# Unscaled keys in a delta-rule recurrence, one written order for all engines, and other places for loads and transposes

## The chip, the core and the metric

The kernel runs on one core of a Trainium2 chip. The core has five engines with a queue of instructions each, worked off in order: TensorE (PE) for matrix products and transposes, VectorE (DVE), ScalarE (ACT) and GpSimd (POOL) for elementwise work, and SyncE (SP), which here does nothing but start transfers (DMAs). An engine that waits holds everything that stands behind in its queue. Matrix products are written to PSUM, eight banks of 2 KB per partition; everything else lies in SBUF. The metric is the device time of one execution in microseconds (us).

## The reference

Two blocks follow each other. The first is a delta-rule attention (4 batches, 8 heads, 768 steps, 48 dimensions per head), the second a feed-forward block with SiLU on 3072 tokens (384 to 2048 to 384). The two weight matrices come as 64-bit floats, all else as 32-bit floats.

```
k_n = k / (np.linalg.norm(k, axis=-1, keepdims=True) + 1e-06)
for t in range(S):
    kt, vt, bt = (k_n[:, :, t], v[:, :, t], beta[:, :, t, None])
    y[:, :, t] = np.einsum('bhd,bhde->bhe', q[:, :, t], state)
    v_old = np.einsum('bhde,bhd->bhe', state, kt)
    state = state + bt[:, :, :, None] * np.einsum('bhd,bhe->bhde', kt, vt - v_old)
...
x = np.ascontiguousarray(attn_out.transpose(0, 2, 1, 3)).reshape(B * S, H * D)
h = x @ w_in
g = h * (1.0 / (1.0 + np.exp(-h)))
return (g @ w_out).astype(np.float32)
```

## The kernel before

**Tiling.** The 768 steps are cut into 6 chunks of 128. A unit is one batch of one chunk (24 units, numbered chunk by chunk): 128 steps on the partitions, 8 heads of 48 dimensions beside each other, padded to 64. For each chunk c the kernel runs these stages over the four units:

- `norms(c)`: ACT squares the keys, DVE sums them and computes the inverse norm by Newton steps (13 small operations on 128x32).
- `scale(i)`: POOL multiplies the keys of unit i by the inverse norm (`kb`) and the result by -beta (`bkb`). POOL has no access to PSUM.
- `turn(i)`: PE transposes `kb` and `qb` (4 transposes each, tile `pt`), DVE and ACT copy them to `kq`.
- `score(i)`: PE multiplies keys by keys and queries (`pa`, 8 matmuls), ACT copies and DVE masks the results, with the scale -beta, to `ap`.
- `block_out(i)`, `block_in(i)`: the 32x32 blocks on the diagonal of the scores go to DRAM and come back regrouped (`g`, 128 blocks on the partitions).
- `invert(c)`: a recurrence on DVE inverts all 128 triangular blocks at once: POOL selects the part above the diagonal of `g` into `x`, and 30 steps of two operations (`rank`, `x`) follow; then the results go through DRAM (`up`, `low`) to the tiles `xe` and `xi`.
- `solve(c)`: PE merges the 32x32 inverses to 64x64 (`py`, `px`), solves for the new values (`pz`, first half, across, second half), updates the state (`pu`) and forms the attention output (`pyc`). ACT and DVE move results between PSUM and SBUF in each step (`y`, `xi`, `z`, `vf`, `xT`).
- `feed_forward(c)`: `hidden` (`phid`, 6 matmuls per step, SiLU to `gT` on ACT) and `project` (`po`, 16 matmuls per batch), both over the finished chunk. `go(pieces, n)` puts n small pieces of it between steps of the next chunk's stages.

**Weights.** Each of the two matrices is fetched raw in eight pieces of 0.79 MB into rooms that are free for the moment (`fetch_w_in`, `fetch_w_out`). `narrow` turns the 64-bit words of a piece to 32-bit floats: ACT takes Abs and Identity of the two halves, DVE does three operations, and POOL adds. A queue of pieces and `fill(n)` spread these operations over the first chunk. The raw pieces of `w_out` 2, 3, 6 and 7 share buffers (tag `ap`) with the scores.

**Order.** A scheduler would order the queues by itself. Two helpers bind it: `in_line` chains all DMAs on SP in program order, and `pin` chains an engine's operations in program order, but only once the engine stands in `pins`: for DVE, PE and POOL after the first weight pieces, for ACT never. `busy` is a matmul without use (`pw`), run so that PE is not idle.

**Start.** SP loads beta, 4 key units and 3 query units, then four pieces of `w_in` between the block transfers of chunk 0. Pieces 4 to 7 follow the first loads of v and are in flight during `invert(0)`. The keys of chunk 1 are loaded behind `invert(0)`, their norms and transposes come during and after `solve(0)`.

The lines below carry the numbers that the profile uses.

Of the kernel before, what the change touches and what calls it, by code (L numbers as in the profile page):

```python
# [21 lines left out]
def kernel(  # L22
# [9 lines left out]
):  # L32

# [9 lines left out]
    nc = tc.nc  # L43
# [42 lines left out]
    def pin(op):  # L86


        engine = op.ins.engine
        if engine in pins:  # L90
            behind(op, pins[engine])
            pins[engine] = op
        return op
# [13 lines left out]
    NQ, NK, NBK = 3, 2, 5  # L107
# [3 lines left out]
    kfs, vfs, invs = {}, {}, {}  # L111
# [8 lines left out]
    def load_k(i):  # L120
        if i < N:
            kfs[i] = load.tile([P, H, D], FP32, name="kf", bufs=5)
            in_line(nc.sync.dma_start(out=kfs[i][:], in_=chunk_of(k, i)))
# [11 lines left out]
    pin(nc.vector.memset(seen[:], 0.0))  # L135
    states = [const.tile([P, NP, 2 * W], FP32, name=f"state{b}") for b in range(B)]
    pin(nc.vector.memset(states[B - 1][:], 0.0))
    for t in qbufs:
        pin(nc.vector.memset(t[:, :, :, D:W], 0.0))
    beta_fm = work.tile([BH, S], FP32, name="beta_fm", tag="ap", bufs=4)  # L140
    in_line(nc.sync.dma_start(out=beta_fm[:], in_=beta.rearrange("b h s -> (b h) s")))
    for load_one, i in (
        *((load_k, i) for i in range(B)), *((load_q, i) for i in range(NQ)),
    ):
        load_one(i)
# [104 lines left out]
    for t in kbufs + bkbufs:  # L250
        nc.gpsimd.memset(t[:, :, :, D:W], 0.0)
# [14 lines left out]
    zbufs = [const.tile([P, NP, 2, W], FP32, name=f"z{i}") for i in range(3)]  # L266
# [17 lines left out]
    nc.scalar.activation(out=seen[:], in_=seen[:], func=ACTF.Silu)  # L284

    beta_tok = const.tile([P, NCH, BH], FP32, name="beta_tok")
    turned = None
    for c in range(NCH):
        if c < NCH - 2:
            turned = busy(turned)  # L290
        pb = bank(psM, "m", "pb")
        last = turned
        turned = nc.tensor.transpose(
            pb[:, 0:BH], beta_fm[:, c * C : (c + 1) * C], ident[0:BH, 0:BH]
        )
        if last is not None:
            behind(turned, last)
        pin(nc.scalar.activation(
            out=beta_tok[:, c, :], in_=pb[:, 0:BH], func=ACTF.Copy, scale=-1.0
        ))  # L300


    def norms(c):

        def one(name, dtype=FP32):
            return small.tile([P, BH], dtype, name=name, bufs=1)[:]

        ss = one("ss")
        for b in range(B):
            sq = work.tile([P, H, D], FP32, name="sq", bufs=1)  # L310
            pin(nc.scalar.activation(out=sq[:], in_=kfs[c * B + b][:], func=ACTF.Square))
            pin(nc.vector.tensor_reduce(
                out=ss[:, b * H : (b + 1) * H], in_=sq[:], axis=AX.X, op=ALU.add
            ))
        seed, t, r = one("seed", U32), one("nt"), one("nr")
        inv = small.tile([P, B, H], FP32, name="inv")
        pin(nc.vector.tensor_scalar(
            out=seed, in0=ss.bitcast(U32), scalar1=-0.5, scalar2=1597463007.0,
            op0=ALU.mult, op1=ALU.add,
        ))  # L320
        root = seed.bitcast(FP32)
        for _ in range(3):
            pin(nc.vector.scalar_tensor_tensor(
                out=t, in0=ss, scalar=-0.5, in1=root, op0=ALU.mult, op1=ALU.mult
            ))
            pin(nc.vector.tensor_tensor(out=t, in0=t, in1=root, op=ALU.mult))
            pin(nc.vector.scalar_tensor_tensor(
                out=r, in0=t, scalar=1.5, in1=root, op0=ALU.add, op1=ALU.mult
            ))
            root = r  # L330
        pin(nc.vector.tensor_tensor(out=t, in0=r, in1=ss, op=ALU.mult))
        pin(nc.vector.tensor_scalar(
            out=t, in0=t, scalar1=1e-6, scalar2=-1.0, op0=ALU.add, op1=ALU.mult
        ))
        pin(nc.vector.reciprocal(out=inv[:].rearrange("p b h -> p (b h)"), in_=t))
        for b in range(B):
            invs[c * B + b] = inv[:, b, :]
# [5 lines left out]
    def scale(i):  # L343

        b, c = units[i]
        kb, bkb = kbufs[i % NK], bkbufs[i % NBK]
        bt = beta_tok[:, c, b * H : (b + 1) * H]
        pin(nc.gpsimd.tensor_tensor(  # L348
            out=packed(kb), in0=kfs.pop(i)[:],
            in1=invs.pop(i).unsqueeze(2).to_broadcast([P, H, D]), op=ALU.mult,  # L350
        ))
        scaleds[i] = pin(nc.gpsimd.tensor_tensor(
            out=packed(bkb), in0=packed(kb), in1=bt.unsqueeze(2).to_broadcast([P, H, D]),
            op=ALU.mult,
        ))

    def turn(i, rooms):

        kb, bkb, qb = kbufs[i % NK], bkbufs[i % NBK], qbufs[i % NQ]
        if i not in scaleds:  # L360
            scale(i)
        scaled = scaleds.pop(i)
        kq = work.tile([P, NP, 2, C], FP32, name="kq", bufs=4)
        for j, (src, room) in enumerate(zip((kb, qb), rooms)):
            pt = bank(*room, "pt")
            for p in range(NP):
                pin(nc.tensor.transpose(  # L367
                    pt[:, p * C : (p + 1) * C], src[:, p].rearrange("p e w -> p (e w)"), ident[:]
                ))
            ptv = pt[:].rearrange("p (a t) -> p a t", a=NP)  # L370
            if j == 0:
                pin(nc.vector.tensor_copy(out=kq[:, :, j, :], in_=ptv))  # L372
            else:
                pin(nc.scalar.copy(kq[:, :, j, :], ptv))  # L374
        return dict(kq=kq, bkb=bkb, scaled=scaled)

    def score(i, u, rooms):

        b, c = units[i]
        kq, bt = u["kq"], beta_tok[:, c, b * H : (b + 1) * H]  # L380
        ap = work.tile([P, H, 2, C], FP32, name="ap", tag="ap", bufs=4)
        u["ap"] = ap
        for g, room in enumerate(rooms):
# [29 lines left out]
            u["ends"] = (copied, masked, u["scaled"])  # L413
            yield

    def block_out(i, u):
# [3 lines left out]
        if b == 0:  # L420
            blocks[c] = (
                tc.dram_tile([B, H, NB, T, T], FP32, name=f"blocks{c}"),
                work.tile([P, T, T], FP32, name="g", tag="g", bufs=1),
                work.tile([P, T, T], FP32, name="x", tag="x", bufs=1),
            )
        there = blocks[c][0]
# [12 lines left out]
    def invert(c):  # L439
# [4 lines left out]
        pin(nc.gpsimd.affine_select(  # L444
            out=x[:], in_=g[:], pattern=[[-1, T], [1, T]], compare_op=ALU.is_gt, fill=0.0,
            base=0, channel_multiplier=0,
        ))
        diagonal = x[:].rearrange("p s t -> p (s t)")[:, 0 : T * T : T + 1]
        yield pin(nc.vector.memset(diagonal, 1.0))
# [35 lines left out]
    def solve(c, us):  # L485
# [8 lines left out]
        def z_of(x):  # L494
            return zbufs[(c * B + x) % len(zbufs)]
# [157 lines left out]
        for k in range(B + 3):  # L653
# [3 lines left out]
            if k >= 3:  # L657
                old(k - 3)
                made = [update(k - 3), new(k - 3)]
                for part in made:  # L660
                    next(part, None)
# [12 lines left out]
            for part in made:  # L674
                next(part, None)
# [56 lines left out]
    def prepare(c, us):  # L732

        for b in range(B):
            i = c * B + b
            us.append(turn(i, (A, CC)))
            yield
# [5 lines left out]
            load_k(i + B)  # L743
            yield

    norms(0)
    fetch_w_in(0)
    us = [turn(0, (M, M))]
    load_q(B - 1)
    fetch_w_in(1)  # L750
    for b in range(B):
        if b + 1 < B:
            us.append(turn(b + 1, (M, M)))
        go(score(b, us[b], (CC, A)), 3)
        block_out(b, us[b])
        if b < 2:
            fetch_w_in(2 + b)
# [3 lines left out]
    ends = us[B - 1]["ends"]  # L761
# [28 lines left out]
    begun = fill(5)  # L790
    for op in begun:
        for end in ends:
            if end.ins.engine == op.ins.engine:
                behind(op, end)
    quiet = us[B - 1]["last"]
    for _ in range(16):
        quiet = busy(quiet, NoSync)
    for engine, op in (("vector", begun[-1]),):
        pins[op.ins.engine] = op
    pins[quiet.ins.engine] = quiet  # L800
    pins[adds[-1].ins.engine] = adds[-1]

    for i in range(B):
        load_v(i)
    for i in range(4, NWI):
        fetch_w_in(i)
    fetch_w_out(0)
    for n, done in enumerate(invert(0)):
        if n == 18:
            for i in range(20):  # L810
                busy(done if i == 0 else None, Sync)
# [13 lines left out]
    fill(7)  # L825
    for n in range(B, 2 * B):
        load_k(n)
    more(1, ("in", 1))
    pieces = feed_forward(0)
    for n, _ in enumerate(solve(0, us)):  # L830
        fill(2)
        if n == 5:
            norms(1)
            scale(B)
        if n == 3:
            for i in range(B, B + NQ):
                load_q(i)
            more(2)
            more(3)
        if n == 7:  # L840
            scale(B + 1)
        if n == 8:
            more(4, ("out", 1))
        for _ in range((2, 2, 1, 1, 1, 1, 1)[n] if n < 7 else 0):
# [8 lines left out]
    next_us = []  # L853
# [3 lines left out]
    for n in range(4):  # L857
        go(prep)
        go(pieces, 2)
        fill(3)  # L860
        if n % 2 == 0:
            scale(B + 2 + n // 2)
    for n in range(2):
        until(("out", 6 + n))
        for _ in range(2):
            go(prep)
            go(pieces)
    inv = invert(1)
    for _ in range(20):
# [5 lines left out]
    for n, _ in enumerate(solve(1, us)):  # L875
        go(pieces, 2 if n in (1, 2) else 1)
    norms(2)
# [5 lines left out]
    for c in range(1, NCH):  # L883
        if c + 1 < NCH:
# [13 lines left out]
            if c + 2 < NCH:  # L898
                norms(c + 2)
# [35 lines left out]
```

## Time and profile before

| | us |
|---|---|
| five runs | 801.94, 803.23, 798.36, 801.18, 801.08 |
| median | 801.18 |
| the profiled execution, its own time | 801.94 |
| its span, first to last instruction | 800.2 |
| PE busy | 764.1 (95%) |
| DVE / ACT / POOL busy | 338.6 / 224.1 / 85.4 |
| mean granted clock of PE | 0.98 |
| chain that ended last: PE, issue, DMA, DVE | 86%, 4%, 4%, 2% |
| PE phid / po on that chain | 31% / 30% |

How to read it: the busy time of an engine is the time in which one of its instructions runs; a matrix product overlaps the load of the next weights (PEld), and products are pipelined. One product of 32-bit floats can be two instructions in the trace. The granted clock is the share of full speed at which PE was let run; stretches of it below 1 are slow whatever stands in PE's queue. The chain of waits is followed back from the last instruction to whatever released each step, and printed in order of time. In a timeline, the bracket behind a row gives the idle time of the engine before it and what ended it. Times are counted from the span's start.

### The profile page before, as it was taken

The page shows a single profiled execution, that of the slowest core. Times are in us where ns is not written, and L with a number is a line of the kernel's source. Part 1 is how long each engine was busy: PE and PEld are TensorE (multiplying, and loading weights), DVE is VectorE, ACT ScalarE, POOL GpSimd, SP SyncE. Part 2 cuts the span into 40 slices and gives each one's busy share as a digit, 9 for nine tenths or more (in the row PEclk, how much of TensorE's full clock was granted, in tenths as well). Part 3 has the DMA queues.
Part 4 walks back from the last instruction along what each step waited for, and adds up shares of the span by engine and source line. Part 5 has one row for each costly group of instructions (what it writes and reads, how often), then busy time and mean ns, then how long its engine had stood idle before and what let it go on. Part 6 is the DMA issues. An engine that isn't in the chain of part 4 may idle for free.

```text
span 800.2 us, 15363 instructions
## 1 busy us (share of the span) xinstructions
PE 764.1 (95%) x6344; PEld 573.9 (72%) x6344; DVE 338.6 (42%) x871; ACT 224.1 (28%) x482; POOL 85.4 (11%) x96
## 2 busy tenths in 40 slices
PE   7919798999999999999999999999999999999998
PEld 4505586678768678868778868778868778768684
DVE  3678788392245642325642325642325642100000
ACT  3604437212235113224113225113214113211020
POOL 6003355100020000020000020000020000000000
PEclk9959899999999999999999999999999999999999
DMA  8795536503025140025140025140022040000000
GB/s 156 136 203 149 132 117 160 102 11 95 6 66 104 39 102 2 12 60 104 39 102 3 11 61 103 34 102 8 10 61 52 13 111 4 10 21 1 20 1 20
DMA packets 155061, 50.84 MB, mean 64 GB/s; under 512 B 142544, under 2 KB 147536, under 8 KB 154992
## 3 DMA queue, kind: packets, MB, share of 16 engines
q1 hardware_dynamic: 154992, 49.87, 28.3%
q8 instruction: 50, 0.82, 0.4%
q14 instruction: 19, 0.16, 0.1%
HBM read 34.70 MB, written 14.16 MB: 61 GB/s over the span
## 4 chain that ended last, share of the span: by engine, by line
PE 86%; issue 4%; DMA 4%; DVE 2%; ACT 1%; SPq 1%; POOL 1%; ACTq 0%; DVEq 0%; POOLq 0%
PE phid L687 31%; PE po L707 30%; PE pa L388 5%; PE pz L551 3%; PE pyc L610 3%; PE pt L367 3%; PE pyc L582 2%; PE ph L535 2%; PE pu L593 2%; PE py L518 1%; PE px L518 1%; DMA w_out<-in_moe_w_in_dram 1%; PE pz L559 1%; DMA raw_out<-in_moe_w_out_dram 1%; DVE rank L454 1%
## 5 line engine op out<-in xcount | busy, mean ns | idle before, releaser
L687 PE MATMUL phid<-xT,w_in 128*128 128x256 f32 x1152 | 266.5, 383 | 0.0
L707 PE MATMUL po<-w_out,gT 128*128 128x384 f32 x768 | 254.6, 489 | 0.0
L687 PEld LDWEIGHTS phid<-xT,w_in 128*128 128x128 f32 x1152 | 213.1, 190 | 35.4 <-issue 6.5
L707 PEld LDWEIGHTS po<-w_out,gT 128*128 128x128 f32 x768 | 144.1, 190 | 96.4 <-issue 1.2
L697 ACT ACTIVATE gT<-phid 128x512 f32<-128x512 f32 x96 | 57.3, 597 | 162.0 <-PE phid L687 162.0
L404 DVE SCALAR_TENSOR_TENSOR ap<-pa,beta_tok,above 128x128 f32<-128x128 f32 x192 | 58.2, 377 | 51.4 <-ACT ap L398 51.4
L275 PE MATMUL pw<-state,ident 128*128 128x384 f32 x98 | 41.6, 572 | 22.2 <-DVE x L458 17.2
L454 DVE TENSOR_TENSOR rank<-g,x 128x30 f32<-128x30 f32 (+9 forms) x180 | 59.7, 332 | 6.1
L458 DVE TENSOR_TENSOR x<-x,rank 128x30 f32<-128x30 f32 (+9 forms) x180 | 59.6, 331 | 6.3 <-DVE rank L454 0.2
L348 POOL TENSOR_TENSOR kb<-kf,inv 128x384 f32<-128x384 f32 x24 | 20.2, 842 | 364.1 <-PE po L707 240.3
L713 ACT ACTIVATE o<-po 128x384 f32<-128x384 f32 x24 | 11.8, 490 | 158.1 <-PE po L707 158.0
L388 PE MATMUL pa<-kq 48*128 48x256 f32 x384 | 49.6, 394 | 4.3 <-ACT kq L374 3.5
L398 ACT ACTIVATE ap<-pa,beta_tok 128x128 f32<-128x128 f32 x144 | 41.5, 367 | 31.4 <-PE pa L388 31.4
L388 PEld LDWEIGHTS pa<-kq 48*128 48x128 f32 x384 | 36.4, 189 | 16.0 <-issue 7.5
L275 PEld LDWEIGHTS pw<-state,ident 128*128 128x128 f32 x98 | 19.9, 216 | 34.8 <-issue 20.8
L551 PEld LDWEIGHTS pz<-vf,xi 64*64 64x64 f32 x768 | 37.0, 137 | 10.6 <-issue 7.8
L542 DVE TENSOR_TENSOR vf<-vf,pz 64x384 f32<-64x384 f32 x24 | 13.4, 558 | 73.4 <-PE pz L551 31.5
L551 PE MATMUL pz<-vf,xi 64*64 64x48 f32 x768 | 41.5, 222 | 1.4 <-DVE vf L542 1.3
L542 DVE TENSOR_TENSOR vf<-vf,ph 128x384 f32<-128x384 f32 x20 | 11.1, 554 | 51.6 <-PE ph L535 51.3
L372 DVE COPY kq<-pt 128x512 f32<-128x512 f32 x24 | 16.4, 683 | 35.9 <-PE pt L367 35.8
L569 ACT COPY z<-pz 64x384 f32<-64x384 f32 x48 | 22.7, 472 | 31.6 <-PE pz L551 17.5
L559 PE MATMUL pz<-z,ap 64*64 64x48 f32 x384 | 27.8, 223 | 0.0
(98 smaller groups left out, 588.1 us busy)
## 6 DMA issues: line engine op xcount, KB each, us to landing
kf<-in_k_dram SPq DMA_DIRECT2D x24, 192.0 KB, 3.1
qb<-in_q_dram SPq DMA_DIRECT2D x24, 192.0 KB, 3.5
vf<-in_v_dram SPq DMA_DIRECT2D x24, 192.0 KB, 3.5
out_dram<-o SPq DMA_DIRECT2D x24, 192.0 KB, 1.9
blocks<-ap SPq DMA_DIRECT2D x96, 32.0 KB, 1.7
g<-blocks SPq DMA_DIRECT2D x24, 128.0 KB, 2.7
up<-x SPq DMA_DIRECT2D x6, 512.0 KB, 2.6
low<-g SPq DMA_DIRECT2D x6, 512.0 KB, 2.8
```

The costliest lines, as they stand in the source:

```text
L275: done = pin(nc.tensor.matmul(pw[:, 0:DM], lhsT=ident[:], rhs=states[B - 1][:].rearrange("p a w -> p (a w)")[:, 0:DM], start=True, stop=Tr ...
L388: u["last"] = pin(nc.tensor.matmul(pa[e][:, pp * 2 * C : (pp + 1) * 2 * C], lhsT=kq[rows, 2 * g + pp, 0, :], rhs=kq[rows, 2 * g + pp, :, : ...
L398: copied = pin(nc.scalar.activation(out=ap[:, h, 0, :], in_=pa[e][:, at : at + C], func=ACTF.Copy, scale=bt[:, h : h + 1],))
L404: masked = pin(nc.vector.scalar_tensor_tensor(out=ap[:, h, j:2, :], in0=pa[e][:, at + j * C : at + 2 * C].rearrange("p (j t) -> p j t", j= ...
L454: pin(nc.vector.tensor_tensor(out=tv, in0=g[:, 0:m, m : m + 1].to_broadcast([P, m, n]), in1=x[:, m : m + 1, m + 1 : T].to_broadcast([P, m, ...
L458: yield pin(nc.vector.tensor_tensor(out=x[:, 0:m, m + 1 : T], in0=x[:, 0:m, m + 1 : T], in1=tv, op=ALU.add))
L542: pin(nc.vector.tensor_tensor(out=vs[x][rows], in0=vs[x][rows], in1=what[rows], op=ALU.add))
L551: yield pin(nc.tensor.matmul(pzs[x][rows, h, :], lhsT=xis[x // HB][rows, x % HB * H + h, :], rhs=vs[x][rows, h, :], start=True, stop=True,))
L559: yield pin(nc.tensor.matmul(pzs[x][hi, h, :], lhsT=us[x]["ap"][lo, h, 0, W:C], rhs=z_of(x)[lo, h // 2, h % 2, 0:D], start=True, stop=True,))
L687: pin(nc.tensor.matmul(ph[:, j * GT : (j + 1) * GT], lhsT=w_in[:, a, (2 * f + j) * P : (2 * f + j + 1) * P], rhs=xTs[c, hf][:, a, :], star ...
L697: pin(nc.scalar.activation(out=gTs[f // FG][:, f % FG, :], in_=ph[:], func=ACTF.Silu, scale=0.5))
L707: pin(nc.tensor.matmul(po[:, 0:DM], lhsT=gTs[f // 2 // FG][:, f // 2 % FG, at : at + C], rhs=w_outs[f // HFF][:, f % HFF, :], start=(f == ...
```

## The change

The keys stay unscaled. With n the norm (plus 1e-6) and g = -beta/n², the scores of raw keys are scaled by g; the state and the solved values are those of the scaled problem times n, so v is multiplied by n (`size`, POOL), the keys by g for the update (`scale`, POOL), and q enters with the sign turned. Transposes then need only the loaded keys, which are loaded straight into padded buffers (`kbufs`, five; `qbufs`, four; `zbufs`, four, which also hold the squares).

All engines are pinned from the first instruction, ACT included. Chunk 0 starts with three `busy` matmuls and the transposes of two units; beta of chunk 0 alone is transposed there. In `invert`, POOL fills `x` with zeros and ones ahead of time, and three copies on DVE and two on ACT bring in the part of `g` that the first steps need, in the place of POOL's selection and a write of the diagonal.

SP has a new order: all of chunk 0's keys and queries, `w_in` pieces 0 and 1, the blocks of chunk 0 without a break, then the keys of chunk 1, pieces 2 and 3, the queries of chunk 1, v, the transfers of `invert(0)`, and only then pieces 4 to 7. The betas of chunks 1 to 5 and the transposes of chunk 1 stand on PE in `invert(0)`, ahead of the 20 `busy` matmuls; for chunks 0 and 1 ACT alone copies them to `kq`. `squares(1)` and `norms(1)` follow `invert(0)` directly instead of running in `solve(0)`. In `solve`, the products `pu` and `pyc` of a step come behind its `pz` products. `solve(0)` has 13 `busy` matmuls instead of 9, and more pieces of `feed_forward(0)` are spent before `invert(1)` begins.

```diff
     def pin(op):
         engine = op.ins.engine
         if engine in pins:
             behind(op, pins[engine])
-            pins[engine] = op
+        pins[engine] = op
         return op
...
-    NQ, NK, NBK = 3, 2, 5
+    NQ, NK, NBK = 4, 5, 5
...
-            kfs[i] = load.tile([P, H, D], FP32, name="kf", bufs=5)
-            in_line(nc.sync.dma_start(out=kfs[i][:], in_=chunk_of(k, i)))
+            in_line(nc.sync.dma_start(out=packed(kbufs[i % NK]), in_=chunk_of(k, i)))
...
+    def squares(c):
+        sums[c] = small.tile([P, BH], FP32, name="ss", bufs=1)[:]
+        for b in range(B):
+            sq = packed(zbufs[b])
+            pin(nc.scalar.activation(
+                out=sq, in_=packed(kbufs[(c * B + b) % NK]), func=ACTF.Square
+            ))
+            pin(nc.vector.tensor_reduce(
+                out=sums[c][:, b * H : (b + 1) * H], in_=sq, axis=AX.X, op=ALU.add
+            ))
...
+        pin(nc.vector.tensor_scalar(out=n[:], in0=t, scalar1=1e-6, scalar2=None, op0=ALU.add))
+        pin(nc.vector.reciprocal(out=r, in_=n[:]))
+        pin(nc.vector.tensor_tensor(out=t, in0=r, in1=beta_tok[:, c, :], op=ALU.mult))
+        pin(nc.vector.scalar_tensor_tensor(
+            out=g[:], in0=r, scalar=-1.0, in1=t, op0=ALU.mult, op1=ALU.mult
+        ))
...
     def scale(i):
+        scaleds[i] = pin(nc.gpsimd.tensor_tensor(
+            out=packed(bkbufs[i % NBK]), in0=packed(kbufs[i % NK]),
+            in1=steps[c][:, b * H : (b + 1) * H].unsqueeze(2).to_broadcast([P, H, D]), op=ALU.mult,
+        ))
+    def size(i):
         pin(nc.gpsimd.tensor_tensor(
+            out=vfs[i][:], in0=vfs[i][:],
+            in1=sizes[c][:, b * H : (b + 1) * H].unsqueeze(2).to_broadcast([P, H, D]), op=ALU.mult,
+        ))
...
-            if j == 0:
+            if j == 1:
+                pin(nc.scalar.mul(kq[:, :, j, :], ptv, -1.0))
+            elif c <= 1:
+                pin(nc.scalar.copy(kq[:, :, j, :], ptv))
+            else:
                 pin(nc.vector.tensor_copy(out=kq[:, :, j, :], in_=ptv))
-            else:
-                pin(nc.scalar.copy(kq[:, :, j, :], ptv))
...
-        pin(nc.gpsimd.affine_select(
-            out=x[:], in_=g[:], pattern=[[-1, T], [1, T]], compare_op=ALU.is_gt, fill=0.0,
-            base=0, channel_multiplier=0,
-        ))
+            if n < T // 4:
+                done = pin(nc.vector.tensor_copy(out=squares_of(x), in_=squares_of(g)))
+            else:
+                pin(nc.scalar.copy(squares_of(x), squares_of(g)))
...
                 made = [update(k - 3), new(k - 3)]
-                for part in made:
-                    next(part, None)
             together(*(
...
-            for part in made:
-                next(part, None)
+            for _ in range(2):
+                for part in made:
+                    next(part, None)
...
+    for b in range(B):
+        scale(b)
+    for i in range(B, 2 * B):
+        load_k(i)
+    fetch_w_in(2)
+    fetch_w_in(3)
+    for i in range(B, 2 * B):
+        load_q(i)
...
+    fill(5)
+    for _ in range(4):
+        busy()
     for i in range(B):
         load_v(i)
+    next_us = []
+    for n, done in enumerate(invert(0)):
+        if n == 1:
+            for c in range(1, NCH):
+                beta_of(c)
+        if n in (3, 5, 7, 9):
+            next_us.append(list(turn(B + len(next_us), M, M))[0])
+        if n == 18:
+            for i in range(20):
+                busy(done if i == 0 else None, Sync)
     for i in range(4, NWI):
         fetch_w_in(i)
     fetch_w_out(0)
-    for n, done in enumerate(invert(0)):
-        if n == 18:
-            for i in range(20):
-                busy(done if i == 0 else None, Sync)
+    squares(1)
+    norms(1)
...
-    fill(7)
+    fill(3)
+    for b in range(B):
+        size(b)
...
-        if n == 5:
-            norms(1)
-            scale(B)
...
-        for _ in range((2, 2, 1, 1, 1, 1, 1)[n] if n < 7 else 0):
+        for _ in range((3, 3, 2, 2, 1, 1, 1)[n] if n < 7 else 0):
             busy()
...
-    for n in range(4):
-        go(prep)
-        go(pieces, 2)
-        fill(3)
-        if n % 2 == 0:
-            scale(B + 2 + n // 2)
-    for n in range(2):
-        until(("out", 6 + n))
-        for _ in range(2):
-            go(prep)
-            go(pieces)
+    for n in range(2):
+        go(prep)
+        go(pieces, 3)
+        fill(6)
+    for n in range(2):
+        until(("out", 6 + n))
+        go(prep)
+        go(pieces, 2)
     inv = invert(1)
+    go(pieces, 6)
```

## The prediction, made before the result was known

> **What bounds the kernel now.** I read the page first. TensorE (PE) is busy for 764 of 800 us, so the question is where the other 36 us and the slow stretches lie. The table of stretches answers it (us, then busy us of PE, PE weight loads, VectorE DVE, ScalarE ACT, GpSimd POOL; the granted clock; the DMA share; GB/s):
>
> ```profile
> 45.00:50.00 5.00, 0.00 (x0) 0.00 (x0) 4.55 (x14) 0.40 (x1) 0.00 (x0) 0.50 1.09 189
> 90.00:95.00 5.00, 4.80 (x40) 3.72 (x42) 3.33 (x4) 1.58 (x4) 2.65 (x2) 0.50 0.02 5
> 145.00:200.00 55.00, 55.00 (x475) 41.10 (x473) 28.18 (x79) 10.96 (x22) 1.26 (x1) 1.00 0.30 66
> 500.00:600.00 100.00, 100.00 (x934) 75.65 (x933) 38.70 (x106) 21.97 (x45) 6.19 (x7) 1.00 0.19 43
> ```
>
> From 145 us PE has no gap at the full clock: what comes earlier there moves the end one for one, and whatever another engine does faster is worth nothing. Before 145 us PE waits, or runs at clock 0.50. The chain of waits shows for what (start, us, what):
>
> ```profile
> 24.61 5.77 DMA w_out<-in_moe_w_in_dram
> 30.39 5.03 DMA w_out<-in_moe_w_in_dram
> 36.83 1.67 DMA blocks<-ap
> 65.95 3.45 DMA low<-g
> 72.44 3.86 DMA xe<-low
> 104.66 2.79 PE phid L687 x12
> ```
>
> The score blocks of chunk 0 wait on SP behind weight transfers from 24.6 to 35.4 us, only then does the recurrence run. The timeline rows of DVE, then PE, carry the durations I use (start, us, instruction, idle before):
>
> ```profile
> 42.81 0.20 DVE L454 TENSOR_TENSOR rank<-g,x 128x30 f32<-128x30 f32 x1
> 64.53 0.19 DVE L458 TENSOR_TENSOR x<-x,rank 128x30 f32<-128x30 f32 x1
> 66.87 1.97 DVE L173 TENSOR_SCALAR w_in<-w_in 128x768 uint32<-128x768 uint32 x1
> 97.33 0.55 DVE L312 TENSOR_REDUCE ss<-sq 128x8 f32<-128x384 f32 x1 [3.32 <-ACT sq L311]
> ```
>
> ```profile
> 56.55 9.92 PE L275 MATMUL pw<-state,ident 128*128 128x384 f32 x21 [17.19 <-DVE x L458]
> 104.59 2.86 PE L687 MATMUL phid<-xT,w_in 128*128 128x256 f32 x12
> 122.87 2.00 PE L388 MATMUL pa<-kq 48*128 48x256 f32 x16 [1.47 <-ACT kq L374]
> 132.62 2.00 PE L388 MATMUL pa<-kq 48*128 48x256 f32 x16 [1.50 <-ACT kq L374]
> 140.24 2.00 PE L388 MATMUL pa<-kq 48*128 48x256 f32 x16 [0.66 <-DVE kq L372]
> ```
>
> The recurrence is 42.8 to 64.7 us; norms(1) sits in the middle of the solve; three waits for kq cost PE 3.63 us.
>
> **The change, part by part** (from the order of instructions on each engine and rows above).
>
> *First scores.* Raw keys are transposed without waiting for norms and scaling (first transposes 12.84 us before). After: three fillers of 1.6 us from 2.7 us, then four cold groups of four transposes (1.0 each) and beta's 0.3 reach 11.7 us. ACT's first score copy followed the first score matmul by 1.87 us (16.70 to 18.57), DVE's first mask by 2.6: 14.1 us. Four units of 2.42 us on DVE follow; in between ACT owes 1.7 of copies and, twice, 1.16 of kq copies, so units start at 14.1, 16.7, 19.6 and 22.0, ending at 24.4 (30.6 before).
>
> *Blocks.* Weight pieces 2 and 3 now stand on SP behind the last block read. Four block writes (1.8), 1.4 to the read's issue (37.28 to 38.66) and 2.67 to its arrival (38.66 to 41.33) give 30.3. POOL's select (1.26) becomes a zero fill done earlier plus small copies, 0.6: the recurrence starts at 30.9, 11.9 earlier, and with its 22.0 us ends at 52.8. The two extra ACT copies lie beside DVE's three.
>
> *Behind it.* PE must now transpose chunk 1 in the recurrence, in order before the 20 fillers. Its loads stand behind weight pieces: from 28 us, 3.15 MB at the 200 GB/s of saturated stretches (171 to 221) land at 45 to 47. Fillers then start at 47, not at 44.7 where the recurrence alone would release them, and with their 16 us (56.55 to 72.53) end at 63.5. The first merge matmul, possible at 52.8+7.8=60.6, waits 3 us.
>
> *Weights.* Pieces 4 to 7 were fetched during the recurrence; they now follow the xi transfers on SP, whose last issue is 12.0 us after the recurrence: 64.8. At 3.9 us per 0.79 MB the first lands at 71. ACT, now in program order, has its Abs (0.9) ahead of the xi copy: 72.4 against 80.38. The lead has shrunk from 11.9 to 8 us.
>
> *Solve.* Before, 23.5 us lie between the first pz (81.10) and phid (104.59): DVE has norms(1) from 92.28 to 102.50, with idle stretches of 3.32, 0.99 and 0.64, and PE is at half clock. norms(1) moves to 54 to 60 us, beside the xe and xi transfers (two more small operations, 0.23 each, hidden there; without the cover 6 us). Walking pz to xT with the row durations, z copies 0.47, Abs and Identity 0.9 and 1.0 in ACT's order, and a weight piece every 3.9 us gives 15.6 us at full clock. At half clock its matmuls and four fillers cost up to 6 more; I take 2, the nearest row (90 to 95 us) being half clock in a part only. phid starts at 74+15.6+2=91.6, 13.0 earlier.
>
> The row is that PE fell to 0.50 at 90 us after gaps of only 1.32 and 1.22 us. The Trainium skill, "TensorE: Matmul & The Clock Gate", Why this matters for your kernels, asks only for no gap above about 3 us. By that rule the 2 us would be nothing and the sum 2 us lower; the row differs, so I keep them.
>
> *From phid to project.* Before: 104.59 to 147.75, 43.2 us. Gone are 4 times 0.87 us of chunk 1's transposes (3.5) and the 3.63 us of waits: 36.0. What is late next is weight conversion, four operations behind. Each weight piece costs DVE 2.1 to 2.3 us, or 2.8 to 3.6 when a POOL add falls beside it (0.69 becomes 1.97 in the row above), and the ap buffers of units 2 and 3 wait for POOL's adds of w_out 6 and 7. My walk puts those at 124.6 and 127.5 us; PE, which would be at unit 3's scores by 122, loses some 5 us there (0 if conversion keeps up, 10 if the last w_out transfers come 5 us later). Project's second matmul ends at 91.6+36+5=132.6: a lead of 15.1.
>
> *Chunk 1 to 2.* Before, 14 project matmuls (9.3 us) followed the last pyc and hid norms(2). The new count of FFN steps leaves 6 (3.9). PE then has transposes and half a phid, 1.6, until 5.5 us after pyc, while DVE needs 1.4 (xT) + 2.3 (sums) + 3.5 (15 small operations) + 0.7 (kq): 7.9. PE waits 2.4 us. Bounds: 0 (squares without the single sq buffer may be quicker) to 4. Later chunks keep 14 project matmuls (9.3+1.6 against 7.9): 0.
>
> *The rest at nothing.* POOL still does two 0.83 us products per unit (keys by g, v by n instead of kb and bkb), in POOL's hundreds of idle microseconds; update and new after the inner products leave the same PE work between dependent steps (2.9 us against 1.0 of copies). Without that cover, up to 0.5 us per chunk. The products of v for chunk 0 stand on POOL behind the add of weight piece 1 (due at 61 to 63, after norms(1) on DVE): four times 0.83 end at 66.5, ahead of the first pz at 74 that waits for them; an add 8 us later would hold the solve. Packed key loads: 3.5 instead of 3.1 us, like q, hidden after chunk 0.
>
> Sum against the profiled execution (801.94, its span 800.2 and 1.7 around): 801.94-15.1+2.4=789.2. The median, 801.18, lies 0.76 lower: 788.4.
>
> **The rivals.**
> - *Conversion and transfers pace it.* For: pieces 4 to 7 and all of w_out start 20 us later on SP, and DVE was busy some 90% from 65 to 140 us already. Against: DVE idles less without norms(1). At 150 GB/s chunk 1's loads land 5 us later and pieces come every 5.2 us: a lead of 8: 801.2-8+2.4=795.6, up to 798 with 10 us of buffer waits.
> - *Everything overlaps.* No half clock (2), no buffer wait (5), no wait at chunk 2 (2.4): 779.
> - *Slower.* One mechanism: the twelve weight pieces from 64.8 us on come one after another and gate ACT, which holds z, xT and gT behind them. With about 13 us from the last one to project, 64.8+12s+13 exceeds 145.3 (147.75-2.4) from s=5.6 us on, a rate of 140 GB/s. Rows of 112 and 123 GB/s exist (70 to 80 us), though there DMA was idle for a third. At 120 GB/s s=6.6: 813.
> - *It does nothing.* Half clock through the whole solve costs 6 instead of 2, buffers 10 instead of 5, and loads 4 us later 4: 788.4+4+5+4=801. Against: the solve's fillers rise from nine to thirteen.
>
> **How the numbers follow.** 788 (own range 782 to 794): 0.53. Paced: 0.20. Overlapped: 0.12. Slower: 0.10. Nothing: 0.05. From 777 to 799 less than 2 in 10 is left out. About 0.3% (2.4 us) is what a measurement tells from no change: faster 0.85 (first three), same 0.04, slower 0.11.
>
> **What would show it.** Right: first rank at 30 to 32 us; w_in of weight pieces 4 to 7 landing after 70; xi copy on ACT right behind an Abs; no ss rows between pz rows; first phid near 92; PE waiting in the third and fourth group of pa rows, then at chunk 2's first pa; PE without gaps afterwards. Wrong: a first rank after 36, phid after 100, or PE gaps per chunk beyond chunk 2.

## The result and the profile after

Practically no change: 801.88 us against 801.98 (medians of 53 and 95 executions), ratio 0.999 (0.998 to 0.9999). The profiled execution took 799.65 us (span 797.9), 2.3 less than the one of before. The steps of the prediction can be followed in it:

| us from the start | before | predicted | after |
|---|---|---|---|
| last mask of chunk 0's scores ends | 30.6 | 24.4 | 27.1 |
| recurrence of chunk 0 starts (first rank) | 42.8 | 30.9 | 34.8 |
| first merge matmul (`py`) | 72.5 | 63.5 | 68.2 |
| `xi` copy on ACT | 80.4 | 72.4 | 77.8 |
| first `pz` | 81.1 | 74 | 78.5 |
| first `phid` | 104.6 | 91.6 | 98.9 |
| project's second matmul done, scores of chunk 1 done | 147.75 | 132.6 | 143.3 |
| own time | 801.94 | 789.2 | 799.65 |

(143.3: `po` begins at 141.94, and two products take 1.34 us by the row of 13 records in 4.36 us.) Every step came earlier than before; of the 12 us at the recurrence 8 were real, 4.5 are left at project, and 2.3 at the end.

The table of stretches of the kernel after, with the columns of before (busy us of PE, PEld, DVE, ACT, POOL; granted clock; DMA share; GB/s):

```profile
10.00:15.00 5.00, 4.42 (x25) 2.98 (x23) 3.69 (x17) 2.30 (x6) 1.90 (x3) 0.68 1.23 178
15.00:20.00 5.00, 5.00 (x28) 3.94 (x27) 2.01 (x8) 3.10 (x10) 1.28 (x2) 0.63 1.09 181
...
45.00:50.00 5.00, 0.26 (x1) 0.27 (x2) 4.58 (x13) 0.00 (x0) 0.00 (x0) 0.50 1.33 158
90.00:95.00 5.00, 4.64 (x66) 4.05 (x63) 2.91 (x5) 1.65 (x6) 0.56 (x1) 0.66 0.49 187
125.00:130.00 5.00, 2.74 (x13) 1.88 (x13) 4.89 (x11) 3.85 (x10) 3.45 (x3) 0.79 0.75 206
130.00:135.00 5.00, 5.00 (x17) 3.60 (x15) 4.90 (x6) 2.15 (x4) 3.33 (x3) 0.53 0.74 146
...
145.00:200.00 55.00, 53.96 (x463) 40.29 (x462) 25.14 (x72) 9.55 (x17) 1.11 (x2) 1.00 0.24 57
...
500.00:600.00 100.00, 100.00 (x937) 75.73 (x936) 41.47 (x117) 23.45 (x51) 7.45 (x10) 1.00 0.18 43
```

Outside chunk 0's recurrence the reader sees three stretches at a lower clock where before had one (10 to 20 and 125 to 135 us are new, 90 to 95 was there), and PE no longer full between 145 and 200 us. The chain of waits (start, us, what):

```profile
31.88 2.40 DMA g<-blocks
58.10 3.21 DMA low<-g
69.01 7.75 DMA raw<-in_moe_w_in_dram
76.78 9.22 DMA raw<-in_moe_w_in_dram
98.94 2.86 PE phid L702 x12
112.50 4.32 DMA w_out<-in_moe_w_out_dram
123.19 5.49 DMA blocks<-ap
...
147.57 2.45 DMA g<-blocks
174.14 10.63 PE phid L702 x48
```

Two things are new on it: raw weight pieces (69 to 86 us), and behind project the blocks and the recurrence of chunk 1, which end at 174 us. DVE now has 7% of the chain, PE 79%; before it was 2% and 86%, with no recurrence of chunk 1 on it. The timeline of DVE, PE and ACT at these places (start, us, instruction, idle before):

```profile
34.78 0.20 DVE L470 TENSOR_TENSOR rank<-g,x 128x30 f32<-128x30 f32 x1
...
56.71 0.19 DVE L474 TENSOR_TENSOR x<-x,rank 128x30 f32<-128x30 f32 x1
```

```profile
49.74 1.12 PE L369 MATMUL pt<-ident,qb 128*128 128x128 f32 x4 [13.00 <-DMA qb<-in_q_dram]
...
55.18 13.07 PE L274 MATMUL pw<-state,ident 128*128 128x384 f32 x40
...
98.94 2.86 PE L702 MATMUL phid<-xT,w_in 128*128 128x256 f32 x12 [0.58 <-ACT xT L643]
...
128.37 3.75 PE L392 MATMUL pa<-kq 48*128 48x256 f32 x14 [2.26 <-ACT ap L402]
...
174.14 10.63 PE L702 MATMUL phid<-xT,w_in 128*128 128x256 f32 x48 [1.04 <-ACT gT L712]
```

```profile
76.92 0.90 ACT L164 ACTIVATE w_in<-raw 128x768 f32<-128x768 f32 x1 [2.62 <-DMA raw<-in_moe_w_in_dram]
77.84 0.57 ACT L539 COPY xi<-px 32x512 f32<-32x512 f32 x1
...
172.52 1.08 ACT L478 COPY g<-x 128x512 f32<-128x512 f32 x1 [3.96 <-DVE x L474]
173.51 1.07 ACT L712 ACTIVATE gT<-phid 128x512 f32<-128x512 f32 x2
```

PE stood 13 us for a query of chunk 1; the 20 fillers behind its transposes then held the merge until 68.2, although the recurrence had ended at 56.9 and xe needs some 7 us from there (its transfer is issued at 61.3 and lands within 2.8 us). ACT's Abs of weight piece 4 held the `xi` copy. At 172.5 ACT made its half of the copy of g in chunk 1's `invert`, when the recurrence allowed it; the activations for gT stood behind it in ACT's queue, and PE behind these. This last wait is in no step of the prediction. In the kernel before, four activations for gT came between the second `o` of project and this copy, in the changed kernel two (165.37 and 167.96). ACT waited for the copy there too, but PE had no gap (the timeline of ACT in the kernel before):

```profile
177.82 0.60 ACT L697 ACTIVATE gT<-phid 128x512 f32<-128x512 f32 x1 [2.05 <-PE phid L687]
179.72 1.10 ACT L462 COPY g<-x 128x512 f32<-128x512 f32 x1 [1.30 <-DVE x L458]
```

### The profile page after: what moved, and what is told of

Read it like the earlier page. It is cut to its first block, busy times and chain, and to the rows that moved or that the text cites. A ratio compares the mean times of both kernels' runs of the same rounds, so it can differ in the third digit from the quotient of the medians.

```text
span 797.9 us, 15397 instructions
## 1 busy us (share of the span) xinstructions
PE 759.9 (95%) x6326; PEld 572.1 (72%) x6326; DVE 339.3 (43%) x892; ACT 231.1 (29%) x502; POOL 82.6 (10%) x102
## 4 chain that ended last, share of the span: by engine, by line
PE 79%; DVE 7%; DMA 6%; SPq 3%; ACT 2%; issue 1%; POOL 0%; ACTq 0%; DVEq 0%
PE phid L702 29%; PE po L722 28%; PE pa L392 5%; PE pz L567 3%; DVE x L474 3%; DVE rank L470 3%; PE pyc L626 2%; PE ph L551 2%; DMA raw<-in_moe_w_in_dram 2%; PE pt L369 2%; PE pyc L598 2%; DMA blocks<-ap 1%; PE px L534 1%; PE py L534 1%; PE pu L609 1%
## 5 line engine op out<-in xcount | busy, mean ns | idle before, releaser
L408 DVE SCALAR_TENSOR_TENSOR ap<-pa,g,above 128x128 f32<-128x128 f32 x192 | 58.2, 377 | 46.2 <-ACT ap L402 45.8
L392 PE MATMUL pa<-kq 48*128 48x256 f32 x384 | 55.3, 415 | 4.4 <-ACT ap L402 2.5
L402 ACT ACTIVATE ap<-pa,g 128x128 f32<-128x128 f32 x144 | 41.6, 366 | 37.9 <-PE pa L392 33.8
L392 PEld LDWEIGHTS pa<-kq 48*128 48x128 f32 x384 | 39.3, 199 | 17.9 <-issue 9.6
L345 POOL TENSOR_TENSOR bkb<-kb,g 128x384 f32<-128x384 f32 x24 | 19.9, 833 | 222.3 <-issue 159.3
L274 PE MATMUL pw<-state,ident 128*128 128x384 f32 x80 | 30.4, 525 | 4.4 <-DVE state L139 2.8
L369 PE MATMUL pt<-ident,qb 128*128 128x128 f32 x96 | 16.1, 294 | 14.4 <-DMA qb<-in_q_dram 14.4
L626 PE MATMUL pyc<-ap,z 128*64 128x128 f32 x368 | 26.6, 279 | 0.0
```

Of the source, the lines that this page charges most:

```text
L274: done = pin(nc.tensor.matmul(pw[:, 0:DM], lhsT=ident[:], rhs=states[B - 1][:].rearrange("p a w -> p (a w)")[:, 0:DM], start=True, stop=Tr ...
L369: pin(nc.tensor.transpose(pt[:, p * C : (p + 1) * C], src[:, p].rearrange("p e w -> p (e w)"), ident[:]))
L392: u["last"] = pin(nc.tensor.matmul(pa[e][:, pp * 2 * C : (pp + 1) * 2 * C], lhsT=kq[rows, 2 * g + pp, 0, :], rhs=kq[rows, 2 * g + pp, :, : ...
L402: copied = pin(nc.scalar.activation(out=ap[:, h, 0, :], in_=pa[e][:, at : at + C], func=ACTF.Copy, scale=bt[:, h : h + 1],))
L408: masked = pin(nc.vector.scalar_tensor_tensor(out=ap[:, h, j:2, :], in0=pa[e][:, at + j * C : at + 2 * C].rearrange("p (j t) -> p j t", j= ...
L626: pin(nc.tensor.matmul(pys[x][at], lhsT=z[:, p, e, :], rhs=ap[:, 2 * p + e, 1, :], start=(c == 0), stop=(c > 0), skip_group_check=True,))
```

## The experiments

The questions were where the lead of 8 us shrank, and whether more lead would have reached the end. Theory A: transfers pace what lies before the solve. B: PE's own order does. C: the conversion on DVE and POOL is the bound from 100 to 141 us. D: score buffers and the half clock there. E: the clock at the start. G: ACT's written order behind project. Ratios are against the kernel before, run beside each.

**Queries of chunk 1 first.**

```diff
+    for i in range(B, 2 * B):
+        load_q(i)
     fetch_w_in(2)
     fetch_w_in(3)
-    for i in range(B, 2 * B):
-        load_q(i)
```

> Chunk 1's queries are loaded ahead of weight pieces 2 and 3. Theory A (transfers pace it: in the changed kernel the wait for qb held the transposes, and so the 20 fillers, until 55 us, but weight pieces 4 to 7, issued behind xi at 67.5 us, gate ACT after that): the transposes end before 48 us, the first merge matmul comes at 64.5 to 66 instead of 68.2, but the xi copy still follows the Abs of raw piece 4 at 76 to 78, and the time stays within 2 us of the changed kernel's 801.9. Theory B (PE's order alone delays it: fillers behind late transposes): the 3.4 us are kept to the end, 798 to 799. Theory C (VectorE's conversion work from 104 to 141 us is the bound): no change, 801 to 803.

799.17 us, ratio 0.9956 (0.9931 to 0.9981). The timeline of PE, then of ACT:

```profile
40.06 1.12 PE L369 MATMUL pt<-ident,qb 128*128 128x128 f32 x4 [3.52 <-DMA qb<-in_q_dram]
48.46 14.74 PE L274 MATMUL pw<-state,ident 128*128 128x384 f32 x40 [2.12 <-DVE x L474]
```

```profile
76.50 0.89 ACT L164 ACTIVATE w_in<-raw 128x768 f32<-128x768 f32 x1 [5.79 <-DMA raw<-in_moe_w_in_dram]
77.41 0.57 ACT L539 COPY xi<-px 32x512 f32<-32x512 f32 x1
```

The merge began 5.0 us earlier (63.2), but the `xi` copy only 0.4: what PE gained, ACT waited for at the next weight piece (5.79 instead of 2.62 us). In the traces phid (97.7) and the end (796.8) are 1.2 and 1.1 us earlier, as A has it; the medians differ by 2.7, nearer to B's number. The trace decides for A on the mechanism.

**Pieces 4 to 7 back ahead of the recurrence's transfers.**

```diff
+        if n == 1: ...
+            for i in range(4, 8):
+                fetch_w_in(i)
...
-    for i in range(4, NWI):
-        fetch_w_in(i)
     fetch_w_out(0)
```

> Weight pieces 4 to 7 stand again behind v, ahead of the transfers that follow the recurrence, as in the kernel before. Theory A: 3.15 MB at 160 to 190 GB/s more lie ahead of the transfers up, low and xe; they are issued at 67 us instead of 57, the first merge matmul comes at 75 to 78 instead of 68.2, the xi copy at 83 to 86 instead of 77.8; no Abs waits for a DMA any more. The time rises by 4 to 8 us, to 806 to 810. Theory C (conversion on VectorE is the bound, wherever the pieces land): within 2 us of 801.9, since VectorE then has its pieces early. Theory B: like A, as far as the merge is late.

810.37 us, ratio 1.0097 (1.0058 to 1.0135): 8.5 above the changed kernel. The timeline of PE:

```profile
76.91 0.31 PE L534 MATMUL py<-xe,ap 32*32 32x32 f32 x2 [10.18 <-DMA xe<-low]
```

Theory A: SP's issue of `up` moved to 65.9, xe came at 76.9, the `xi` copy at 88.4. The copy and the time lie just above A's ranges (83 to 86, 806 to 810). The place behind the recurrence was thus right for this kernel; what it costs there is the wait of ACT.

**Queries between the blocks, one piece ahead.**

```diff
         block_out(b, us[b])
+        load_q(B + b)
...
+            fetch_w_in(4)      # in invert(0), behind v
```

> Chunk 1's queries go between the block transfers of chunk 0, where the DMA engines moved only 70 GB/s (20 to 30 us), and weight piece 4 behind v, ahead of the transfers of the recurrence. Theory A: the last block read is at most 1 us later, the transposes end by 48 us, the first merge matmul comes at 64.5 to 66, the Abs of piece 4 waits for nothing, the xi copy comes at 72 to 74 instead of 77.8, and the last piece of w_in at 90 to 91 instead of 95: 5 us earlier at phid, 795 to 798. Theory B: 3.4 us, 798 to 799. Theory C: VectorE is full from 104 to 141 us whatever comes earlier, so at most 1 to 2 us are kept: 799.5 to 802.

797.95 us, ratio 0.9943 (0.9926 to 0.9961). The timeline of ACT:

```profile
72.29 0.90 ACT L164 ACTIVATE w_in<-raw 128x768 f32<-128x768 f32 x1
74.06 0.57 ACT L539 COPY xi<-px 32x512 f32<-32x512 f32 x1 [0.86 <-PE px L534]
```

The recurrence began 1.3 us later (36.1), yet with the piece there the `xi` copy came at 74.1, phid at 95.2 and the end at 794.8, 3.7 and 3.1 earlier. Theory A holds before the solve. C's bound (1 to 2 us) is refuted as stated: the conversions after 100 us started earlier too.

**A small addition on POOL.**

```diff
-        out=to.bitcast(I32), in0=to.bitcast(I32), in1=low.bitcast(I32), op=ALU.add
+        out=to[:, 0:1, 0:8].bitcast(I32), ...
```

> POOL's last addition of each weight piece covers 8 elements per partition instead of 768, so the weights come out wrong in their last bits and everything else stays. It takes away POOL's 1.84 us per piece and the lengthening of VectorE's conversions beside it. Those conversions that lay beside an addition took up to 1.95 to 2.25 us instead of 0.56 to 0.69: 12.6 us in all, 8.6 of them after 104 us. Theory C: the stretch from the first phid (98.9) to project (143) shrinks from 44 to 35 to 37 us and the time falls by 7 to 9 us, to 793 to 795. Theory A: transfers keep the pace until 95 us, and after it the waits of ACT and of the score buffers for POOL's additions go, 2 to 4 us: 798 to 800. Theory B: nothing, 801 to 803.

797.32 us, ratio 0.9936 (0.9910 to 0.9963). The timeline of DVE, first of the changed kernel, then of this one:

```profile
107.04 1.88 DVE L166 TENSOR_SCALAR w_out<-w_out 128x768 f32<-128x768 f32 x1 [0.64 <-ACT w_out L164]
...
114.99 2.09 DVE L172 TENSOR_SCALAR w_out<-w_out 128x768 uint32<-128x768 uint32 x1
```

```profile
111.42 0.56 DVE L166 TENSOR_SCALAR w_out<-w_out 128x768 f32<-128x768 f32 x1 [0.65 <-ACT w_out L164]
...
114.94 0.56 DVE L172 TENSOR_SCALAR w_out<-w_out 128x768 uint32<-128x768 uint32 x1
```

From phid (103.3 in this trace) to project it took 38.8 us instead of 44.3, counted as in the table: 5.5 us less, where C expected 7 to 9. In the whole time a part of this was hidden by a solve at clock 0.50 from 85 to 95 us, which made phid 4.4 us late. The median, 797.32, lies between C's range (793 to 795) and A's (798 to 800). Conversion and POOL's additions do hold this stretch, C and D together.

**Fillers between the first transposes.**

```diff
     for t in turning:
         next(t)
+        for _ in range(2):
+            busy()
```

> Two more fillers behind each of the two q transposes of the start (four in all, 0.7 us each at full clock). Of four executions of this start so far two had the granted clock at 0.53 to 0.79 from 10 to 20 us, and the last mask at 27 us, and two had 1.00 and 24.2 us. Theory E (the short transposes with gaps between them lose the clock): with the fillers the clock is 1.00 from 10 to 20 us, the last mask ends at 24.5 to 26, and the time falls by 0 to 1.5 us, since behind it the transfers hold most of it. Rival (the clock is lost by chance, whatever stands there): clock and last mask as scattered as before, the time the 2.8 us of fillers later at the first scores, 802 to 804.

798.05 us, ratio 0.9958 (0.9943 to 0.9973). The table of stretches:

```profile
10.00:15.00 5.00, 5.00 (x31) 3.25 (x28) 2.52 (x13) 1.85 (x5) 1.91 (x3) 1.00 1.23 171
15.00:20.00 5.00, 5.00 (x42) 4.05 (x42) 4.47 (x16) 4.77 (x14) 1.29 (x2) 1.00 1.08 172
```

The last mask ended at 25.7. The clock was 1.00 at this place in all four traces that have these fillers; of the nine traces with the start as in the changed kernel, five had 1.00 and the last mask at 24.2 to 24.6, four 0.53 to 0.79 and 26.8 to 27.1. In the trace the gain is 1.4 us, in the median 3.8, more than E expected: the times now lie within 797.0 to 799.4 instead of 795.8 to 808. Where the changed kernel's median execution loses 2.2 us against its traced one no trace shows; it stays open.

**Scores of units 2 and 3 later in PE's order.**

```diff
-        go(pieces, 3)
+        go(pieces, 4)
         fill(6)
     for n in range(2):
         until(("out", 6 + n))
-        go(prep)
-        go(pieces, 2)
+        go(pieces, 2 + 2 * n)
+        go(prep)
     inv = invert(1)
-    go(pieces, 6)
+    go(pieces, 2)
```

> The changed kernel with the scores of chunk 1's units 2 and 3 put later in PE's order: behind 16 instead of 12 steps of phid, and with four steps of project between them. Nothing is added or removed. Theory D (the wait of 2.26 us for ap at 126 us and the half clock after it, 5.4 us on pa and phid rows, are lost because PE's order meets ACT's copies too early, while VectorE's conversions go on): the pa waits and the half clock at 126 to 135 us go, project begins at 134 to 136 instead of 142, and 4 to 8 us are kept: 794 to 798. Theory C (the conversion of w_out itself holds project): PE waits for the additions of w_out 6 and 7, at 135 and 138 us, in the first po group instead, and at most 0 to 2 us are kept: 800 to 802.

803.62 us, ratio 1.0021 (0.9997 to 1.0044). The timeline of PE, then of ACT:

```profile
126.36 2.83 PE L702 MATMUL phid<-xT,w_in 128*128 128x256 f32 x12 [2.90 <-ACT gT L712]
...
170.47 13.60 PE L702 MATMUL phid<-xT,w_in 128*128 128x256 f32 x48 [6.03 <-ACT gT L712]
```

```profile
168.85 1.06 ACT L478 COPY g<-x 128x512 f32<-128x512 f32 x1 [8.96 <-DVE x L474]
169.82 1.08 ACT L712 ACTIVATE gT<-phid 128x512 f32<-128x512 f32 x2
```

The pa waits and the half clock at 130 us went, as D has it: from phid to project it took 38.9 us instead of 44.3, counted as in the table (12 of the 16 `po` records ahead of the last pa group are taken off, 3.9 us). Then PE stood 6.0 us at 164 to 170 instead of 1.0, at a clock of 0.94 from 145 to 200 us: all was given back. The traced execution is the fastest of the ten (798.92), so the trace shows the order of the waits and not the median. Neither D nor C had this wait. It gave theory G.

**Without the six steps ahead of `invert(1)`.**

```diff
     inv = invert(1)
-    go(pieces, 6)
```

> The changed kernel without the six steps of feed_forward(0) ahead of invert(1); they run behind solve(1) instead, 8.8 us of PE work more to cover squares(2) and norms(2). If the wait of 1.44 us for kq at 234 us and that of 1.04 us for gT come from the missing cover, as the prediction's step from chunk 1 to chunk 2 has it: the kq wait goes and the time falls by 1 to 1.5 us, to 800.4 to 800.9. Rival: PE then reaches solve(1) before xe has landed (it comes at 192 us, 19.5 us after the recurrence's end, 11 us more than the transfers took in chunk 0, so 8.8 us earlier is just covered): 0 to 2 us lost, 802 to 804.

808.23 us, ratio 1.0076 (1.0049 to 1.0102); both expectations missed. The timeline of PE:

```profile
174.20 14.86 PE L702 MATMUL phid<-xT,w_in 128*128 128x256 f32 x60 [8.75 <-ACT o L728]
```

The kq wait of chunk 2 went, as the prediction's step has it, but the 8.8 us of work taken away came back as a wait of 8.75 for the same copy on ACT (`o` stands behind it in the queue). So the changed kernel has at this place just enough PE work for its recurrence.

**The copy of g on DVE alone, in chunk 1** (on top of the later scores).

```diff
-        pin(nc.scalar.copy(g[:, 0:half, :], ...))
+        copy = nc.vector.tensor_copy if c == 1 else nc.scalar.copy
+        pin(copy(g[:, 0:half, :], ...))
```

> The scores of units 2 and 3 later, as before, and one thing more: in chunk 1 the copy of the recurrence's result to g is done by VectorE alone. With the later scores PE began project 4.8 us earlier counted from the first phid, but then waited 6.03 us for gT at 164 to 170 us: ScalarE, in its written order, stood at its half of the copy of g until the recurrence ended at 168.8, with the activations for gT behind it. Theory G (this order takes back whatever PE gains before it): the wait of 6 us goes, the first merge matmul of chunk 1 comes at about 186 instead of 191.4, the time falls by 5 to 6 us against the later scores alone, 797 to 799. Rival (the recurrence's own chain holds chunk 1: xe lands some 8 us after its end, now 0.6 us later): PE waits for xe in place of gT, 0 to 2 us kept, 801.5 to 804.

796.01 us, ratio 0.9920 (0.9889 to 0.9951): 7.6 below the later scores alone. The table of stretches:

```profile
145.00:200.00 55.00, 55.00 (x478) 41.36 (x477) 28.43 (x81) 9.73 (x20) 1.11 (x2) 1.00 0.28 63
```

PE has no gap left there. From the first phid to the first merge of chunk 1, the same PE work in all these kernels, it took 93.2 us in the changed one, 96.0 with the later scores, 86.2 with the copy moved as well. Theory G is shown: the copy's place in ACT's queue made the wait. The gain is above the 5 to 6 us expected; the stretch also ran at clock 1.00 instead of 0.94. That fixing ACT's order put the copy there is not shown, since no run leaves that order to the scheduler.

**Combinations.** Transfers and later scores, with the copy still on ACT:

> The transfers of the third experiment (queries of chunk 1 between the blocks, weight piece 4 behind v) together with the later scores of units 2 and 3. Theory A and D both: the two gains lie one behind the other and add up, 3.5 to 4 and 4 to 8: 790 to 794. If conversion on VectorE holds project (theory C): the later scores bring nothing on top, 797 to 799.

800.04 us, ratio 0.9985 (0.9967 to 1.0003). PE waited 6.3 us for gT; on top of the transfers (797.95) the later scores brought nothing and cost 2.1. C had expected that they bring nothing (797 to 799), but the reason is G's. All together (fillers, transfers, scores, copy):

> All together: the four fillers at the start, queries of chunk 1 between the blocks and weight piece 4 behind v, the later scores of units 2 and 3, and the copy of g on VectorE in chunk 1. Theory G with A: the transfers' 3.5 us and the scores' 5 us are both kept, and the fillers keep the clock up: 790 to 794. Rival (xe of chunk 1 or another wait holds PE): like the transfers alone, 796 to 799.

790.63 us, ratio 0.9862 (0.9836 to 0.9888), as G with A has it. The same with the scores where they were:

> As the one with all together, but with the scores of units 2 and 3 where the changed kernel has them. Theory G: the wait of 2.2 us for ap at 124 us and the half clock behind it stay, the wait for gT (1.45 us) goes: 794 to 797, 3 to 5 us above the one with all together. If the later scores bring nothing: the same as the one with all together.

795.58 us, ratio 0.9923 (0.9897 to 0.9948): the later scores are worth 5.0 us once ACT's copy is out of the way. And with chunk 2's keys copied by ACT (`elif c <= 2`):

> As the one with all together, and ScalarE instead of VectorE copies the transposed keys of chunk 2 to kq, where PE waited 1.4 us for VectorE (which has the sums and norms of chunk 2 ahead of it). If that order makes the wait: 1.0 to 1.4 us less than the one with all together. Rival (PE then waits for g of norms(2), which the masks need in any case, at the next score buffer): no difference.

789.52 us, ratio 0.9848 (0.9821 to 0.9876). The table of stretches:

```profile
200.00:300.00 100.00, 100.00 (x955) 77.72 (x951) 46.65 (x138) 31.03 (x73) 7.49 (x10) 1.00 0.29 64
```

PE was busy 98.6 us here in all other kernels with the change but the one without the six steps; the wait of 1.44 us is gone. The times alone do not tell the last two kernels apart (their intervals overlap). This version is faster than both kernels, by 1.5% than the one before.

## Why the prediction was wrong

The forecast of 788 (range 777 to 799) missed; the time is that of "it does nothing", to which I gave 0.05.

- **First scores** was right at full clock: 24.2 to 24.6 in five traces against 24.4. The traced execution ran at 0.63 to 0.68 there and lost 2.7 us. I had walked these rows with slow transposes (1.0 us a group) and no term for the clock behind them.
- **Blocks** was 6.5 us from last mask to first rank, and measured 7.7: the last unit's writes began 1.6 us after the mask instead of at once.
- **Behind it** had the mechanism right (loads, transposes, then fillers) and two terms too small: 200 GB/s where the stretches show 158 to 186, so that the wait for queries lasted until 49.7 instead of 45 to 47, and nothing for the transposes behind the late load (5.4 us from there to the fillers, at clock 0.72 from 50 to 55). The fillers took 13.1 us, not 16, which gave 3 us back.
- **Weights** had ACT's order right, a late Abs just ahead of the `xi` copy, and its size wrong: the first piece landed at 76.8, not 71, and the pieces' Abs follow each other by 4.6 us, not 3.9. The rival "conversion and transfers pace it" describes this part; the experiments on transfers confirm it.
- **Solve** was 17.6 us from first pz to phid, measured 20.4 (before 23.5): norms(1) is gone as predicted, but PE waits for late pieces and ran at 0.66 from 90 to 95.
- **From phid to project** was 36.0 us of PE work plus 5 for the score buffers; it took 44.3. The cause was POOL's additions, as named, but not only through the score buffers: at the longest wait they held the Abs of a weight piece that stands ahead of the copies in ACT's queue (rows below). It cost 2.8 us of idle time and two things not priced. A pa group that a wait breaks in two takes 2.97 us instead of 2.00 at full clock, three times: 2.9. Half clock behind the longest wait took 2.8 more (pa 3.75 instead of 2.27, phid 4.16 instead of 2.86). So of the 5.4 us that theory D put down to the clock about half were breaks. The timeline of ACT in the changed kernel:

```profile
126.15 0.91 ACT L164 ACTIVATE w_out<-raw_out 128x768 f32<-128x768 f32 x1 [3.69 <-POOL w_out L180]
135.00 1.66 ACT L402 ACTIVATE ap<-pa,g 128x128 f32<-128x128 f32 x6 [2.85 <-POOL w_out L180]
```

- **Chunk 1 to 2**: 2.4 predicted, 1.44 measured (0.19 in before at this place), by the mechanism named; the order on ACT removes it.
- **Where the lead of 15.1 us went**: 4.5 was left at project. Of the 10.7 missing, 4.5 are gone at the first pz (the weight pieces and what stands ahead of them), 2.8 in the solve and 3.4 from phid to project. By size the forecast failed here: the mechanisms were near, these terms of the sum were too small. The prediction's own signs of being wrong (first rank after 36, phid after 100) did not show, at 34.8 and 98.9, although at phid 5.7 of the predicted lead of 13.0 was left.
- **The step whose mechanism failed** is the sentence ahead of the sum: "what comes earlier there moves the end one for one". It took a full PE in before as proof that nothing else was near. Behind project stands ACT's copy of g, tied to chunk 1's recurrence, which began 7.3 us earlier than before (150.4 against 157.7). With PE 4.5 us earlier, 1.04 us were lost there in the traced execution; the later scores show that 5 us more lead would have been lost almost whole. The step "the rest at nothing" had looked at `invert`'s new small copies, not at the copy that ACT, now in written order, reaches before gT.

At the end of the profiled executions the sum closes: 4.5 at project, less 1.04 for gT, less 1.25 more for kq, is 2.2; the own times differ by 2.3. That the medians differ by 0.1 goes with the clock, though no trace shows in which stretch: over the changed kernel's executions the mean granted clock has the median 0.972 (0.976 in the profiled one), before's 0.981 beside the experiments. Over the executions of the changed kernel 0.001 of clock goes with some 0.5 us. By this the profiled one would lie 2 us below the median, and it does (799.65 to 801.88). That the clock is the cause is not shown. The rival "it does nothing" had two terms that were found, the late loads and the buffers, but its main one, half clock through the whole solve, was not; in the traced execution the low clock came in three short stretches.

## What to carry to other kernels

Follow a lead past the stretch that it is gained in, on every engine's queue: an engine that is never idle in the old profile says nothing on the next wait, and an in-order copy that depends on another engine's long chain holds all that stands behind it. Before reordering, count how much independent work lies between such a copy and what feeds it; here taking 8.8 us of it away made a wait of 8.75. Give a wait of two microseconds on TensorE a second term for the half clock that may follow, and judge by medians of executions, since one trace can differ by more than the gain.

## What was unexpected of the hardware

The same PE instructions from the start ran at different clocks: 10 to 20 us had 1.00 in five traces and 0.53 to 0.79 in four. Nor did the length of a gap decide: behind 2.26 us of waiting the clock fell to 0.53 (130 to 135 us, the changed kernel), behind 2.90 us (later scores) and 2.39 us (copy moved) it stayed at 1.00. With the later scores too, in the kernel with all together, a wait of 2.72 us was followed by 12 phid instructions in 4.51 us instead of 2.83. The Trainium skill, "TensorE: Matmul & The Clock Gate", Part 1: The HAM clock gate, says that the window in which activity is counted runs freely and does not restart with the kernel, so that the number of slow products at the start varies from run to run. These rows show a scatter of that kind later, from 10 us on. Its rule in "Why this matters for your kernels", no gap above about 3 us, does not protect here: the clock fell behind 2.26 us.
